# Gated recurrent attention and a two-layer MLP: batches in pairs, every engine on one written-out order, weights loaded later

## The chip, the cores and the metric

One core of one Trainium2 chip. The metric is the device time of one execution in microseconds; the median of several executions is compared. Engines: TensorE (PE, with its weight loads as PEld), VectorE (DVE), ScalarE (ACT), GpSimd (POOL), and SyncE (SP), which here only issues DMAs.

## The reference

A gated linear attention over 4 batches, 8 heads, 768 steps and head width 48, then a leaky-ReLU MLP over the 3072 tokens:

```python
f = 1.0 / (1.0 + np.exp(-f_logit))
for t in range(S):
    state = f[:, :, t, :, None] * state + np.einsum('bhd,bhe->bhde', k[:, :, t], v[:, :, t])
    y[:, :, t] = np.einsum('bhd,bhde->bhe', q[:, :, t], state)
x = np.ascontiguousarray(y.transpose(0, 2, 1, 3)).reshape(B * S, H * D)
h = x @ w_in                      # 384 -> 2048
out = np.maximum(0.01 * h, h) @ w_out   # 2048 -> 384
```

## The kernel before

The recurrence is cut into 6 chunks of 128 steps. A unit is one chunk of one batch with all 8 heads: 128 tokens of width 384, so 24 units, chunk by chunk and in each chunk batch by batch. Inside a chunk the gates become running sums, so that the recurrence turns into matrix products plus one state per batch that goes from chunk to chunk (`state_f` in float32, `state_b` in bf16).

One unit passes through these steps; the names are the functions of the code. `load` issues four 192 KB DMAs (f, k, q, v) on SP. `gate_act` computes log(1 + exp(-f)) on ScalarE; `gate_pe` forms the running sums by a product with a triangle of ones (tile cs); `decay_act` takes exp of plus and minus the sums on ScalarE (em_t, a_t) and the chunk's end factor (a_end). `scale_pool` multiplies k and q by these on POOL (kh, qh) and casts v to bf16 in two layouts. `turn_pe` transposes kh and qh on TensorE into one PSUM tile, and `turn_dve` copies them out (kT, qT). `score_pe` forms k against q per head (tiles pw), `mask_dve` multiplies them by the triangle (wm), and `mix_pe` adds the products with the old state and with v into py, which `y_dve` copies out as xT. `state_pe`, `state_dve` and `state_pool` bring the state forward. The MLP of the unit is `up` (in four groups g of 12 products with 128 columns, each followed by a leaky ReLU on ScalarE into gT), `down` (16 products with 384 columns) and `put` (copy out on VectorE, store on SP).

Each engine works off its own queue in the order in which the code issues to it; the scheduler does not reorder (`manual_schedule`). In turn i of the main loop TensorE gets, in this order: the turns of unit i+1, up groups 0 and 1 of unit i, the scores of unit i+1, the running sums of unit i+2, up groups 2 and 3 of unit i, mix and state of unit i+1, down of unit i. Loads run five units ahead. The weights (w_in in six DMAs, w_out in two, cast to bf16 on the way) are issued on POOL's queue at the start, before the first unit has arrived. PSUM: two banks for up, one for down, one for the turns, two for the scores, two for the rest.

Of the kernel before, what the change touches and what calls it, by code (L numbers as in the profile page):

```python
# [15 lines left out]
def kernel(  # L16
# [21 lines left out]
    units = [(c, b) for c in range(NCH) for b in range(B)]  # L38
    NU = len(units)
# [3 lines left out]
    work = ctx.enter_context(tc.tile_pool(name="work", bufs=3))  # L43
    gpool = ctx.enter_context(tc.tile_pool(name="gpool", bufs=5))
# [10 lines left out]
    nc.scalar.preload_act_table_set("natural_log_exp_and_others")  # L55

# [5 lines left out]
    nc.gpsimd.memset(ones_col, 1.0)  # L62

    w_in_b = const.tile([128, NK, FF], BF16, tag="w_in")
    w_out_b = const.tile([128, NF, KD], BF16, tag="w_out")


    lfs = [const.tile([128, H, 64], BF16, name=f"lf{i}", tag=f"lf{i}") for i in range(3)]
    qhs = [const.tile([128, H, 64], BF16, name=f"qh{i}", tag=f"qh{i}") for i in range(3)]
    khs = [const.tile([128, H, 64], BF16, name=f"kh{i}", tag=f"kh{i}") for i in range(3)]  # L70
    v2s = [const.tile([128, P2, 4, 16], BF16, name=f"v2{i}", tag=f"v2{i}") for i in range(3)]
    state_f = [const.tile([128, P2, D], FP32, name=f"sf{b}", tag=f"sf{b}") for b in range(B)]
    state_b = [const.tile([128, P2, 2 * D], BF16, name=f"sb{b}", tag=f"sb{b}") for b in range(B)]
    for t in lfs + qhs + khs + v2s + state_b:
        nc.vector.memset(t, 0.0)
    for t in state_f:
        nc.vector.memset(t, 0.0)


    raw = {}  # L80

    def load(u):
        c, b = units[u]
        r = {}
        for name, src in (("f", f_logit), ("k", k), ("q", q), ("v", v)):
            t = inp.tile([128, H, D], FP32, name=f"{name}_raw", tag=f"{name}_raw")
            nc.sync.dma_start(out=t, in_=src[b, :, c * C:(c + 1) * C, :].rearrange("h t d -> t h d"))
            r[name] = t
        raw[u] = r

    def load_w_in(part, parts):
        w = FF // parts
        for kk in range(NK):
            nc.gpsimd.dma_start(out=w_in_b[:, kk, part * w:(part + 1) * w],  # L94
                                in_=moe_w_in[kk * 128:(kk + 1) * 128, part * w:(part + 1) * w])

    def load_w_out(part, parts):
        n = NF // parts
        nc.gpsimd.dma_start(  # L99
            out=w_out_b[:, part * n:(part + 1) * n, :],  # L100
            in_=moe_w_out[part * n * 128:(part + 1) * n * 128, :].rearrange("(a p) n -> p a n", p=128))

    st = {}


    def gate_act(u):
        f = raw[u]["f"]
        e = work.tile([128, H, D], FP32, name="e_t", tag="e_t")
        nc.scalar.activation(e, f, AF.Exp, scale=-1.0)  # L109
        lf = lfs[u % 3]  # L110
        nc.scalar.activation(lf[:, :, 0:D], e, AF.Ln, bias=1.0)  # L111

    def gate_pe(u):
        c, b = units[u]
        lf = lfs[u % 3]
        cs = ps_s.tile([128, 512], FP32, name="cs", tag="sm")
        nc.tensor.matmul(cs[:, 0:H * D], ut, lf[:, :, 0:D], start=True, stop=True)  # L117
        if c < NCH - 1:
            for p in range(P2):
                nc.tensor.matmul(cs[:, H * D + p:H * D + p + 1], lf[:, 2 * p:2 * p + 2, :], ones_col,  # L120
                                 start=True, stop=True)
        st[u] = {"cs": cs}

    def decay_act(u):
        c, b = units[u]
        cs = st[u]["cs"]
        a_t = work.tile([128, H, D], BF16, name="a_t", tag="a_t")
        em_t = work.tile([128, H, D], BF16, name="em_t", tag="em_t")
        nc.scalar.activation(em_t, cs[:, 0:H * D], AF.Exp, scale=1.0)  # L129
        nc.scalar.activation(a_t, cs[:, 0:H * D], AF.Exp, scale=-1.0)  # L130
        if c < NCH - 1:
            a_end = work.tile([128, P2], FP32, name="a_end", tag="a_end")
            nc.scalar.activation(a_end, cs[:, H * D:H * D + P2], AF.Exp, scale=-1.0)
            st[u]["a_end"] = a_end
        st[u]["a"], st[u]["em"] = a_t, em_t

    def scale_pool(u):
        r = raw.pop(u)
        nc.gpsimd.tensor_mul(khs[u % 3][:, :, 0:D], r["k"], st[u]["em"])  # L139
        nc.gpsimd.tensor_mul(qhs[u % 3][:, :, 0:D], r["q"], st[u]["a"])  # L140
        v_b = work.tile([128, H, D], BF16, name="v_b", tag="v_b")
        nc.gpsimd.tensor_copy(out=v_b, in_=r["v"])  # L142
        v2 = v2s[u % 3]
        nc.gpsimd.tensor_copy(
            out=v2[:, :, 0:4:3, :],
            in_=r["v"].rearrange("t (p j) d -> t p (j d)", j=2)[:, :, 32:64].rearrange("t p (j e) -> t p j e", j=2))
        st[u]["v"], st[u]["v2"] = v_b, v2

    def turn_pe(u):
        tp = ps_t.tile([128, 2, P2, 128], BF16, name="tp", tag="tp")  # L150
        for i, src in enumerate((khs[u % 3], qhs[u % 3])):
            for p in range(P2):
                nc.tensor.transpose(tp[:, i, p, :], src[:, 2 * p:2 * p + 2, :], ident)  # L153
        st[u]["tp"] = tp

    def turn_dve(u):
        tp = st[u].pop("tp")
        kT = work.tile([128, P2, 128], BF16, name="kT", tag="kT")
        nc.vector.tensor_copy(out=kT, in_=tp[:, 0])  # L159
        qT = work.tile([128, P2, 128], BF16, name="qT", tag="qT")  # L160
        nc.vector.tensor_copy(out=qT, in_=tp[:, 1])  # L161
        st[u]["kT"], st[u]["qT"] = kT, qT

    def score_pe(u):
        kT, qT = st[u].pop("kT"), st[u]["qT"]
        pws = [ps_w.tile([128, P2, 128], FP32, name="pw", tag="pw") for j in range(2)]
        for p in range(P2):
            for j in range(2):
                rows = slice(64 * j, 64 * j + D)
                nc.tensor.matmul(pws[j][:, p, :], kT[rows, p, :], qT[rows, p, :], start=True, stop=True)  # L170
        st[u]["pw"] = pws

    def mask_dve(u):
        st[u]["wm"] = []
        for pw in st[u].pop("pw"):
            wm = work.tile([128, P2, 128], BF16, name="wm", tag="wm", bufs=6)
            nc.vector.tensor_mul(wm, pw, ut[:, None, :].to_broadcast([128, P2, 128]))  # L177
            st[u]["wm"].append(wm)
# [3 lines left out]
    def mix_pe(u):  # L182
        c, b = units[u]
        s = st[u]
        qT, v_b, v2, wms = s.pop("qT"), s["v"], s.pop("v2"), s.pop("wm")
        py = ps_s.tile([128, NK, 128], FP32, name="py", tag="sm")
        jobs = []
        if c > 0:
            for g in range(NQ):
                p, i = divmod(g, 3)  # L190
                jobs.append((g, state_b[b][:, p, 32 * i:32 * i + 32], qT[:, p, :]))
        for j in range(2):
            for p in range(P2):
                jobs.append((3 * p + 2 * j, v_b[:, 2 * p + j, 16 * j:16 * j + 32], wms[j][:, p, :]))
            for p in range(P2):
                jobs.append((3 * p + 1, v2[:, p, 2 * j:2 * j + 2, :], wms[j][:, p, :]))
        left = [sum(1 for g, _, _ in jobs if g % 4 == r) for r in range(4)]
        begun = [False] * 4
        for g, lhsT, rhs in jobs:
            kk, r = divmod(g, 4)  # L200
            left[r] -= 1
            nc.tensor.matmul(py[32 * r:32 * r + 32, kk, :], lhsT, rhs, start=not begun[r], stop=left[r] == 0)  # L202
            begun[r] = True
        s["py"] = py

    def state_pe(u):
        c, b = units[u]
        if c == NCH - 1:
            return
        kh, v_b = khs[u % 3], st[u]["v"]  # L210
        pt = ps_s.tile([128, P2, 2 * D], FP32, name="pt", tag="sm")
        for p in range(P2):
            nc.tensor.matmul(pt[:, p, :], kh[:, 2 * p:2 * p + 2, :], v_b[:, 2 * p:2 * p + 2, :],  # L213
                             start=True, stop=True)
        st[u]["pt"] = pt

    def state_dve(u):
        c, b = units[u]
        if c == NCH - 1:
            return  # L220
# [5 lines left out]
    def state_pool(u):  # L226
        c, b = units[u]
        if c == NCH - 1:
            return
# [127 lines left out]
```

## Time and profile before

| | us |
|---|---|
| median of 3 runs | 209.16 (207.51 to 209.66) |
| span of the profiled execution, first to last instruction | 205.0 |
| TensorE busy in the span | 174.8 (85%) |
| ScalarE, VectorE, POOL busy | 99.5, 90.5, 89.1 |

The page gives no time of the profiled execution beside its span; the median of the runs lies 4.16 us above the span. The page divides the span into 40 slices of 5.1 us; a digit is the busy share of a slice in tenths. Matmuls are pipelined and so overlap in the timeline: the length of a group is read from its start to the start of the next.

### The profile page before, as it was taken

The numbers are of one execution on the slowest core, as the hardware profiler recorded it, in microseconds if no ns is written. First come the engines' busy times: TensorE is split into PE (matmuls) and PEld (weight loads), VectorE is DVE, ScalarE is ACT, GpSimd is POOL, SyncE is SP. The second block draws the span as 40 slices with busy tenths as digits, with TensorE's granted clock in tenths as the row PEclk, the third lists the DMA queues.
The fourth block names the chain that finished last, engine by engine and source line by source line (L and its number), as shares of the span: only waits on it lengthen the run. The fifth ranks groups of instructions, "written<-read, shape, count | busy, mean of one in ns | idle before, by whom it ended". The sixth has DMA issues, their size and how long they took to land.

```text
span 205.0 us, 6488 instructions
## 1 busy us (share of the span) xinstructions
PE 174.8 (85%) x2728; PEld 137.1 (67%) x2728; DVE 90.5 (44%) x204; ACT 99.5 (49%) x213; POOL 89.1 (43%) x173
## 2 busy tenths in 40 slices
PE   0000159999999999999999999999999999999993
PEld 0000039778777877877887787788778777877871
DVE  8000046446445444544544454464445455433511
ACT  4000424466447546635744663574476457444440
POOL 8300183663375357337535633743663474134000
PEclk9999999999999999999999999999999999999999
DMA  6999999899979559557755965785696481110111
GB/s 117 167 196 184 194 189 194 145 218 198 187 139 188 109 118 168 123 125 142 163 125 116 180 141 106 146 176 109 109 190 133 104 156 42 42 38 4 42 38 38
DMA packets 106269, 27.16 MB, mean 132 GB/s; under 512 B 100352, under 2 KB 105472, under 8 KB 106240
## 3 DMA queue, kind: packets, MB, share of 16 engines
q1 hardware_dynamic: 103296, 23.60, 58.8%
q0 software_dynamic: 2944, 3.15, 9.2%
q8 instruction: 21, 0.34, 0.7%
q14 instruction: 8, 0.07, 0.1%
HBM read 25.17 MB, written 4.72 MB: 146 GB/s over the span
## 4 chain that ended last, share of the span: by engine, by line
PE 84%; issue 9%; POOL 4%; DVE 1%; POOLq 0%; DVEq 0%
PE pm L250 32%; PE pm L259 31%; PE py L202 6%; PE tp L153 6%; PE pw L170 4%; PE cs L117 3%; PE pt L213 3%; POOL w_in_b L94 2%; POOL w_out_b L99 1%; PE cs L120 1%; DVE wm L177 1%; POOL kh L139 0%; POOL qh L140 0%; DVE osb L264 0%; DVE kT L159 0%
## 5 line engine op out<-in xcount | busy, mean ns | idle before, releaser
L252 ACT ACTIVATE gT<-pm 128x512 bf16<-128x512 f32 x96 | 56.2, 602 | 73.2 <-PE pm L250 71.4
L250 PE MATMUL pm<-xT,w_in_b 128*128 128x128 bf16 x1152 | 73.0, 221 | 0.0
L250 PEld LDWEIGHTS <-w_in_b 128*128 128x128 bf16 x1152 | 66.8, 98 | 0.6
L259 PE MATMUL pm<-w_out_b,gT 128*128 128x384 bf16 x384 | 66.4, 327 | 0.0
L139 POOL TENSOR_TENSOR kh<-k_raw,em_t 128x384 bf16<-128x384 f32 x24 | 21.9, 913 | 92.5 <-issue 62.5
L259 PEld LDWEIGHTS <-gT 128*128 128x128 bf16 x384 | 36.1, 98 | 22.2
L177 DVE TENSOR_TENSOR wm<-pw,ut 128x512 bf16<-128x512 f32 x48 | 30.9, 686 | 22.1 <-PE pw L170 22.1
L264 DVE COPY osb<-pm 128x384 f32<-128x384 f32 x24 | 13.4, 558 | 45.0 <-PE pm L259 45.0
L117 PE MATMUL cs<-lf,ut 128*128 128x384 bf16 x24 | 8.4, 349 | 23.9 <-ACT lf L111 23.9
L109 ACT ACTIVATE e_t<-f_raw 128x384 f32<-128x384 f32 x24 | 12.4, 516 | 23.8 <-DMA f_raw<-in_f_logit_dram 23.8
L238 DVE CAST xT<-py 128x384 bf16<-128x384 f32 x24 | 13.4, 558 | 21.2 <-PE py L202 21.2
L140 POOL TENSOR_TENSOR qh<-q_raw,a_t 128x384 bf16<-128x384 f32 x24 | 22.0, 915 | 0.0
L120 PEld LDWEIGHTS <-lf 128*128 128x128 bf16 x80 | 5.1, 99 | 24.0 <-issue 22.9
L159 DVE COPY kT<-tp 128x512 bf16<-128x512 bf16 x24 | 10.0, 416 | 22.1 <-PE tp L153 22.0
L234 POOL CAST sb<-sf 64x192 bf16<-64x192 f32 x40 | 13.6, 341 | 2.5
L111 ACT ACTIVATE lf<-e_t 128x384 bf16<-128x384 f32 x24 | 12.6, 524 | 0.8
L129 ACT ACTIVATE em_t<-cs 128x384 bf16<-128x384 f32 x24 | 11.8, 490 | 1.7
L142 POOL CAST v_b<-v_raw 128x384 bf16<-128x384 f32 x24 | 12.1, 504 | 0.0
L130 ACT ACTIVATE a_t<-cs 128x384 bf16<-128x384 f32 x24 | 11.7, 486 | 0.0
L231 POOL TENSOR_TENSOR sf<-sf,a_end 128x192 f32<-128x192 f32 x20 | 10.1, 506 | 3.3 <-DVE sf L224 2.2
L170 PE MATMUL pw<-qT,kT 48*128 48x128 bf16 x192 | 9.8, 223 | 0.8 <-DVE qT L161 0.8
L153 PE MATMUL tp<-ident,kh 128*128 128x128 bf16 x96 | 9.7, 227 | 0.8 <-POOL kh L139 0.8
(37 smaller groups left out, 133.1 us busy)
## 6 DMA issues: line engine op xcount, KB each, us to landing
f_raw<-in_f_logit_dram SPq DMA_DIRECT2D x24, 192.0 KB, 3.3
k_raw<-in_k_dram SPq DMA_DIRECT2D x24, 192.0 KB, 4.0
q_raw<-in_q_dram SPq DMA_DIRECT2D x24, 192.0 KB, 4.3
v_raw<-in_v_dram SPq DMA_DIRECT2D x24, 192.0 KB, 4.6
out_dram<-osb SPq DMA_DIRECT2D x24, 192.0 KB, 2.0
w_in_b<-in_moe_w_in_dram POOLq DMA_DIRECT2D x6, 256.0 KB, 8.9
w_out_b<-in_moe_w_out_dram POOLq DMA_DIRECT2D x2, 768.0 KB, 18.3
```

Source lines behind the costliest of these rows:

```text
L117: nc.tensor.matmul(cs[:, 0:H * D], ut, lf[:, :, 0:D], start=True, stop=True)
L139: nc.gpsimd.tensor_mul(khs[u % 3][:, :, 0:D], r["k"], st[u]["em"])
L140: nc.gpsimd.tensor_mul(qhs[u % 3][:, :, 0:D], r["q"], st[u]["a"])
L153: nc.tensor.transpose(tp[:, i, p, :], src[:, 2 * p:2 * p + 2, :], ident)
L170: nc.tensor.matmul(pws[j][:, p, :], kT[rows, p, :], qT[rows, p, :], start=True, stop=True)
L177: nc.vector.tensor_mul(wm, pw, ut[:, None, :].to_broadcast([128, P2, 128]))
L234: nc.gpsimd.tensor_copy(out=state_b[b][rows, :, j * D:j * D + D], in_=sf[rows])
L238: nc.vector.tensor_copy(out=xT, in_=st[u].pop("py"))
L250: nc.tensor.matmul(pm[:, i, :], w_in_b[:, kk, ff * 128:(ff + 1) * 128], s["xT"][:, kk, :], start=(kk == 0), stop=(kk == NK - 1))
L252: nc.scalar.activation(s["g"][:, 4 * g:4 * g + 4, :], pm, AF.Prelu, alpha=0.01)
L259: nc.tensor.matmul(s["pm2"], s["g"][:, ff, :], w_out_b[:, ff, :], start=(ff == 0), stop=(ff == NF - 1))
L264: nc.vector.tensor_copy(out=osb, in_=st[u]["pm2"])
```

## The change

Two batches of a chunk form a pair, so that there are 12 pairs in place of 24 units. Up runs on a pair: half as many products, with 256 columns each, in eight groups of six products per pair (two of the sixteen blocks of w_in), each with one leaky ReLU of 128x512 as before. Down keeps its products with 384 columns, in quarters of four products per batch. The attention's products per batch stay as they are; turns of k and of q have a PSUM tile each. Four PSUM banks serve cs, turns, scores, py and state sums by turns, up keeps two banks, down gets two. From pair 4 on, the gates and the products and casts of k, q and v are one instruction for both batches (768 columns). For the first pairs k (three pairs) and q (two pairs) are multiplied on VectorE in place of POOL. `half`, `units` and `once` only choose slices and create tiles at first use; `turn_dma` is defined but not used.

The loops are replaced by one table of words, which is worked off from left to right; each word issues one step (`name_pair_batch` or `name_pair_group`) to its engine, so it sets every engine's order. For example `sc_8_2` issues the scores of both batches of pair 8, `up_7_2` the third up group of pair 7, `dn_7_0_0` the first quarter of down of pair 7's first batch, `mk_8_0_1` one mask on VectorE, `pr` a leaky ReLU, `st` a store.

The weights are issued from the table too (`WI_1`, `WO_2`). Each starts with a one-element copy on POOL out of the v tile of the named pair's second batch, so that POOL gets to the weight DMAs only when that load has landed: the 17th load on SP's queue for w_in, the 25th for w_out. w_in comes in two quarters and a half (nine DMAs), w_out in four quarters. The stores stand in SP's queue among the loads.

```diff
-    units = [(c, b) for c in range(NCH) for b in range(B)]
+    pairs = [(c, h) for c in range(NCH) for h in range(B // 2)]
+    BY_UNIT = 4
+    K_DVE = 3
+    Q_DVE = 2
...
-    ps_o = ctx.enter_context(tc.tile_pool(name="ps_o", bufs=1, space=bass.MemoryType.PSUM))
-    ps_t = ctx.enter_context(tc.tile_pool(name="ps_t", bufs=1, space=bass.MemoryType.PSUM))
-    ps_w = ctx.enter_context(tc.tile_pool(name="ps_w", bufs=2, space=bass.MemoryType.PSUM))
-    ps_s = ctx.enter_context(tc.tile_pool(name="ps_s", bufs=2, space=bass.MemoryType.PSUM))
+    ps_o = ctx.enter_context(tc.tile_pool(name="ps_o", bufs=2, space=bass.MemoryType.PSUM))
+    ps_g = ctx.enter_context(tc.tile_pool(name="ps_g", bufs=4, space=bass.MemoryType.PSUM))
...
+    def weights(which, j):
+
+        nc.gpsimd.tensor_copy(out=gate_w[:, 0:1], in_=raw(j, "v")[0:1, 1, H - 1, D - 1:D])
+        if which == "in":
+            for lo, hi in ((0, FF // 4), (FF // 4, FF // 2), (FF // 2, FF)):
+                for kk in range(NK):
+                    nc.gpsimd.dma_start(out=w_in_b[:, kk, lo:hi], in_=moe_w_in[kk * 128:(kk + 1) * 128, lo:hi])
+        else:
+            n = NF // 4
+            for part in range(4):
+                nc.gpsimd.dma_start(
...
+    def half(j, i):
+        return slice(i, i + 1) if j < BY_UNIT else slice(0, 2)
...
+    def scale_k(j, i):
+        a = half(j, i)
+        eng = nc.vector if j < K_DVE else nc.gpsimd
...
+    def up(j, g):
+        pm = st[j]["pm", g] = ps_m.tile([128, 2, 256], FP32, name="pm", tag="pm")
+        for i in range(2):
+            ff = 2 * g + i
             for kk in range(NK):
-                nc.tensor.matmul(pm[:, i, :], w_in_b[:, kk, ff * 128:(ff + 1) * 128], s["xT"][:, kk, :],
+                nc.tensor.matmul(pm[:, i, :], w_in_b[:, kk, ff * 128:(ff + 1) * 128],
+                                 st[j]["xT"][:, kk].rearrange("t a s -> t (a s)"),
                                  start=(kk == 0), stop=(kk == NK - 1))
...
+    order = """
...
+    q_1_0 mx_0_1 tk_1_0 Lq_2_0 sb_0_1 xt_0_1 tq_1_0 pt_1_0 k_1_1 cs_2_0 Lv_2_0 dec_2_0 q_1_1 WI_1 ck_1_0 cq_1_0 tk_1_1
+    gate_2_1 sf_1_0 tq_1_1 ck_1_1 sc_1_0 cq_1_1 cs_2_1 mk_1_0_0 dec_2_1 mk_1_0_1 sc_1_1 up_0_0 mk_1_1_0 v_1_1 mx_1_0
...
+    k_2_1 q_2_1 pr_1_4 up_0_7 Lv_3_0 dec_3_0 tk_2_1 WO_2 tq_2_1 ck_2_1 up_1_5 cq_2_1 pr_0_7 sc_2_2 pr_1_5 up_1_6
+    gate_3_1 mk_2_0_0 mk_2_0_1 up_1_7 pr_1_6 v_2_1 mk_2_1_0 cs_3_1 pr_1_7 mk_2_1_1 pt_2_1 dec_3_1 dn_0_0_0 sf_2_1
+    mx_2_2 Lf_4_0 dn_1_0_0 xt_2_0 sb_2_0 xt_2_1 dn_0_0_1 sb_2_1 dn_1_0_1 up_2_0 k_3_0 pr_2_0 up_2_1 dn_0_0_2 pr_2_1
...
+    tq_8_1 dn_6_1_3 cq_8_1 up_7_1 ob_6_1 q_9_0 sc_8_2 st_6_1 pr_7_1 up_7_2 mk_8_0_0 dn_7_0_0 mk_8_0_1 pr_7_2 up_7_3
+    mk_8_1_0 pt_8_0 pt_8_1 mk_8_1_1 pr_7_3 up_7_4 sf_8_0 mx_8_2 pr_7_4 sf_8_1 up_7_5 sb_8_0 xt_8_0 dn_7_0_1 xt_8_1
...
+    """
+    for word in order.split():
+        name, *numbers = word.split("_")
+        parts[name](*[int(n) for n in numbers])
```

More of the change, by code (lines that the diff above doesn't have):

```diff
@@ L72 @@
[L72 to L118, printed above, removed]
+    for t in v2s:
+        nc.gpsimd.memset(t[:, :, 1:3, :], 0.0)
@@ new lines, in weights @@
+    def weights(which, j):
[8 more added lines that the diff above has]
+                nc.gpsimd.dma_start(
+                    out=w_out_b[:, part * n:(part + 1) * n, :],
+                    in_=moe_w_out[part * n * 128:(part + 1) * n * 128, :].rearrange("(a p) n -> p a n", p=128))
@@ L164, in score_pe @@
[L164 to L178, printed above, removed]
```

374 lines of the change are left out of this document (204 added, 170 removed).

## The prediction

> **What bounds the kernel now.** First the page's busy shares and slices, then the windows cut at TensorE's first layer product and at its last one.
>
> ```profile
> span 205.0 us, 6488 instructions
> ...
> PE   0000159999999999999999999999999999999993
> ...
> DMA  6999999899979559557755965785696481110111
> ```
> ```profile
> 0.00:31.72 31.72, 4.85 (x55) 3.44 (x56) 7.58 (x27) 6.07 (x13) 11.20 (x25) 1.00 1.06 175
> 31.72:201.67 169.95, 169.91 (x2676) 133.69 (x2674) 82.38 (x177) 93.47 (x200) 77.90 (x148) 1.00 0.63 126
> 201.67:205.00 3.33, 0.00 (x0) 0.00 (x0) 0.56 (x1) 0.00 (x0) 0.00 (x0) 0.87 0.16 59
> ```
>
> The columns after the length are busy times of PE, PEld, DVE, ACT and POOL, the clock, the DMA share and GB/s. The span falls into three parts. For 31.72 us TensorE does almost nothing (4.85) while the DMA is full (1.06). Then it is busy for 169.91 of 169.95 us, and no other engine comes near that (ACT 93.47). Then 3.33 us of copying out and storing. So time can come only from the head, from the length of TensorE's own stream, or from new gaps in it. The chain of waits says of the head that it waits for data:
>
> ```profile
> 6.99 17.87 issue
> ...
> 111.50 1.34 PE pm L250 x24
> ...
> 115.66 2.60 PE pm L259 x16
> ```
>
> The stream of one unit, from the timeline (start, length of the piece):
>
> ```profile
> 111.34 1.50 PE L250 MATMUL pm<-xT,w_in_b 128*128 128x128 bf16 x24
> 112.78 0.40 PE L170 MATMUL pw<-qT,kT 48*128 48x128 bf16 x8
> 113.11 0.34 PE L117 MATMUL cs<-lf,ut 128*128 128x384 bf16 x1
> 113.28 0.24 PE L120 MATMUL cs<-ones_col,lf 128*128 128x1 bf16 x4
> 113.38 1.50 PE L250 MATMUL pm<-xT,w_in_b 128*128 128x128 bf16 x24
> 114.81 0.35 PE L202 MATMUL py<-qT,sb 128*32 128x128 bf16 x12
> 114.99 0.23 PE L202 MATMUL py<-wm,v_b 128*32 128x128 bf16 x4
> ...
> 115.50 2.76 PE L259 MATMUL pm<-w_out_b,gT 128*128 128x384 bf16 x16
> 118.10 0.39 PE L153 MATMUL tp<-ident,kh 128*128 128x128 bf16 x4
> ...
> 118.55 1.50 PE L250 MATMUL pm<-xT,w_in_b 128*128 128x128 bf16 x24
> ```
>
> From start to start: 7.21 us per unit, of which up is 1.44 + 1.43 = 2.87, down 2.60, and all attention 1.74.
>
> **The stream in the changed kernel.** The arithmetic stays. Up has half as many products, each with 256 columns in place of 128. Inside a group one with 128 columns takes 1.34 / 24 = 55.8 ns, one with 384 takes 2.60 / 16 = 162.5 ns; the line between gives 109.2 ns for 256, so a unit's 24 take 2.62 us. Of the 2.87 now, 2 x 1.34 = 2.68 is inside groups and 0.19 is the edge to the score and mix products that follow. Inside the groups 0.06 is gained; the edges come once a pair in place of once a unit (0.10 a unit). The gain lies between 24 x 0.06 = 1.4 us and 24 x 0.25 = 6.0 us; I take 24 x 0.155 = 3.7, since score and mix are issued for two units together from pair 2 on.
>
> Before 31.72 TensorE had done unit 0's attention (1.74 less the 0.18 of the state products that the first chunk lacks) and unit 1's sums and turns (0.27 + 0.45), 2.3 us at the steady price. The first layer group was slow:
>
> ```profile
> 31.72 2.35 PE L250 MATMUL pm<-xT,w_in_b 128*128 128x128 bf16 x24
> ...
> 34.61 1.50 PE L250 MATMUL pm<-xT,w_in_b 128*128 128x128 bf16 x24
> ```
>
> That is 0.85 more than the next at the same granted clock. The whole stream after, without it: 169.95 + 2.3 - 0.85 - 3.7 = 167.7 us.
>
> **The head.** All weights now wait for data: w_in for the 17th load on SP's queue, w_out for the 25th. Prices:
>
> ```profile
> 0.74 0.42 SPq L87 DMA_DIRECT2D f_raw<-in_f_logit_dram  x1
> ...
> 3.77 0.52 ACT L109 ACTIVATE e_t<-f_raw 128x384 f32<-128x384 f32 x1 [1.75 <-DMA f_raw<-in_f_logit_dram]
> 4.25 2.40 SPq L87 DMA_DIRECT2D f_raw<-in_f_logit_dram  x1
> 6.69 7.49 SPq L87 DMA_DIRECT2D k_raw<-in_k_dram  x1
> ...
> 26.75 0.81 SPq L87 DMA_DIRECT2D k_raw<-in_k_dram  x1
> ...
> 33.44 0.96 SPq L87 DMA_DIRECT2D f_raw<-in_f_logit_dram  x1
> ```
> ```profile
> q0 software_dynamic: 2944, 3.15, 9.2%
> ...
> v_raw<-in_v_dram SPq DMA_DIRECT2D x24, 192.0 KB, 4.6
> out_dram<-osb SPq DMA_DIRECT2D x24, 192.0 KB, 2.0
> ```
> ```profile
> L94 POOL DMA_DIRECT2D w_in_b<-in_moe_w_in_dram x6: 548/563/744, 1.8 to 4.6; - x6
> ...
> DMA to landing us min/median/max: 4.6/8.9/11.2
> ```
>
> With the DMA full and little of the weights left, seven loads go in 33.44 - 26.75 us: 0.96 each. The first lands by 3.77. So the 17th lands between 3.77 + 16 x 0.96 = 19.1 and 0.74 + 16 x 0.96 + 4.6 = 20.7; I take 20. The weights are 9.2% of 205.0 = 18.9 us of all 16 DMA engines, 9.4 for each matrix, 2.4 for a quarter. While they flowed, five loads went from 4.25 to 26.75: 4.8 of 22.5 us, so the weights had 79%. A quarter then takes 3.0 us, and lands after one issue (0.56) and some 2 us of latency (the store's 2.0): 20 + 0.6 + 3.0 + 2 = 25.6. By the spread of landings (4.6 to 11.2, for twice the bytes) it lies between 24.6 and 31. So the first up starts at 25.5 instead of 31.72, and behind it lies nearly all the attention of two pairs.
>
> Then w_in's second half lands at 20.6 + 9.4 / 0.79 + 2 = 34.5; up(0,4), ninth of sixteen groups, wants it after 9 x 0.66 plus 2 us of attention at about 33.5, so this costs one. The 25th load needs 2.8 + 25 x 0.96 + 9.4 = 36.2 us of full DMA and lands at about 37.5; w_out's quarters land at 43, 46, 49 and 52. TensorE has finished the ups of pairs 0 and 1 and pair 2's attention at about 42. So down waits some 1 us, then goes at the pace of w_out, the gaps filled in part by pair 2's first ups, and ends both pairs at 52 + 1.3 + 0.2 + 5.2 = 58.7. Done by then: ups of four units 10.5, downs 10.4, attention of six units 6 x 1.74 - 4 x 0.18 = 9.7, half of pair 2's ups 2.6, one unit's turns 0.45: 33.7 us. There remain 167.7 - 33.7 = 134.0, to 192.7; with the tail of 3.33, 196.0 us of span.
>
> SP's stores now stand between loads: st(0,0) holds the later loads until about 56, but by then three pairs and the gate inputs of the fourth are loaded, and afterwards a pair needs 8 x 0.96 = 7.7 us of loads in 14 us of TensorE. This I cost at nothing. In the head VectorE takes over k's products (three pairs) and q's (two) from POOL:
>
> ```profile
> L177 DVE TENSOR_TENSOR wm<-pw,ut 128x512 bf16<-128x512 f32 x48 | 30.9, 686 | 22.1 <-PE pw L170 22.1
> L264 DVE COPY osb<-pm 128x384 f32<-128x384 f32 x24 | 13.4, 558 | 45.0 <-PE pm L259 45.0
> ...
> L139 POOL TENSOR_TENSOR kh<-k_raw,em_t 128x384 bf16<-128x384 f32 x24 | 21.9, 913 | 92.5 <-issue 62.5
> ```
> ```profile
> L109 ACT ACTIVATE e_t<-f_raw 128x384 f32<-128x384 f32 x24 | 12.4, 516 | 23.8 <-DMA f_raw<-in_f_logit_dram 23.8
> ...
> L224 DVE TENSOR_TENSOR sf<-sf,pt 64x192 f32<-64x192 f32 x20 | 7.2, 358 | 0.6
> ```
>
> No row shows that product on VectorE; between 0.51 (the mask's rate, 384 of 512 columns) and POOL's 0.91, I take 0.55, nearest to the 558 ns copy of the same width. Eight of them with copies and masks keep VectorE busy until about 21, inside the wait for w_in, so they cost nothing; at 0.91 they add 8 x 0.36 = 2.9 us and use up most of that cover. From pair 4 on ScalarE's gate comes as two instructions of 768 columns, at most 4 x 0.52 = 2.1 us in one piece, with the relus queued behind them and up's two PSUM banks behind those. The table puts three to five quarters of down (0.65 each) at these places, so I cost it at nothing; without that cover it would be 2.1 - 0.66 = 1.4 us in each of eight pairs.
>
> The windows say how this stands to the runs: the shown median of 209.16 lies 4.16 above the profiled span (the page gives that execution no time of its own), which I carry over: 196.0 + 4.2 = 200.2.
>
> Two rules of the Trainium skill speak against parts of this. In the rows, POOL's six issues of w_in, from 1.8 to 4.6 us, took 563 ns each in the median while VectorE ran memsets, the last but one group among them:
>
> ```profile
> 3.74 0.84 DVE L75 MEMSET sb<- 128x192 uint32 x4
> ```
>
> The Trainium skill (SBUF — State Buffer, Who interferes with whom) says that a VectorE instruction in a two-port mode shuts GpSimd out of a shared port, so that descriptors of its DMAs wait. By that rule the nine issues beside VectorE's copies could each wait for one instruction; the six unhindered issues here do not bear it out, and it stands as the third rival. The first group's 2.35 us is what the skill (TensorE: Matmul & The Clock Gate, Part 1) calls the cold clock, to which an idle window returns the array; by that rule each long wait in the new head costs another 0.85 us, 1 to 2 us in sum, which I leave to the range because the page's clock row reads 1.00 here.
>
> **The rivals.** *The weights come in time*: w_in and w_out take nearly the whole DMA while queued, as in the 7.49 us that one load's issue hung, and down never waits. Then TensorE is dense from 25.5 with four units' attention of 1.74 - 0.18 behind it, less some 0.7 that the table puts later: 25.5 + 167.7 - 5.5 + 3.3 = 191.0, 195.2 as a time. Against it: the 25th load must pass w_in first.
>
> *New gaps in every pair.* TensorE works strictly by the table; mix(j) stands behind four masks that take 4 x 0.645 on VectorE and begin 0.43 after the scores:
>
> ```profile
> 163.22 0.40 PE L170 MATMUL pw<-qT,kT 48*128 48x128 bf16 x8
> ...
> 163.65 1.29 DVE L177 TENSOR_TENSOR wm<-pw,ut 128x512 bf16<-128x512 f32 x2 [0.89 <-PE pw L170]
> ```
>
> Masks are done 3.0 us after the scores begin; the table puts 0.66 of scores and about 3.0 of other groups there (pair 8: three ups, a quarter of down, two state sums), some 0.6 us of slack. If a copy out and the state additions (0.56 + 2 x 0.36 us) regularly fall before the masks, and the four shared PSUM banks stay held as long, the stall with its follow-on is up to 1.28 us a pair: 200.2 + 11 x 1.28 = 214. It decides from 8.9 / 11 = 0.8 us a pair. For it: the kernel before had no wait in 169.95 us to spoil. Against it: VectorE is half idle (82.38 of 169.95).
>
> *The head does not get shorter.* Descriptors or queueing delay both matrices by 4.5 us each way (w_in's median landing 8.9 in place of 4.6), and up gains only the 1.4: 200.2 + 4.5 + 2.3 = 207.0, up to 209 if both delays add in part. The change then does not do what its early attention is for.
>
> **The numbers.** Forecast 0.50, weights in time 0.18, new gaps 0.19, head not shorter 0.13. A change of under 1% (2.1 us) cannot be told from none. Faster: 0.50 + 0.18 = 0.68, plus 0.02 of the third rival's lower half: 0.70. Same: 0.11. Slower: 0.19. The range goes from the stall-free head with the larger up gain (195.2 - 2.3, and some 2 for the spread of the runs, 207.51 to 209.66) = 191 to 211, past the third rival and as far as gaps of 1.0 us a pair.
>
> **What would show it.** The first up before 27 us; up pieces of 0.65 us for six products; down's first group after 41; TensorE dense from about 59 and its last product near 193. Wrong it would be if the windows after 60 us show TensorE under 98% busy (the second rival), if the first up comes after 30 us (the third), or if down follows the ups without a gap (the first).

## The result, and the profile after

| us | before | after |
|---|---|---|
| median, runs of one chip | 208.39 (207.51 to 209.66, 4 runs) | 197.58 (196.56 to 198.10, 4 runs) |
| ratio after / before, 95% interval | | 0.946 [0.940, 0.952] |
| span of the profiled execution | 205.0 | 195.7 |
| time of that execution | not given | 197.44 |

Faster by 10.8 us; forecast were 200.2 us of time and 196.0 of span. Ratios leave out executions that took over 1.5% longer than the fastest of their kernel, so a ratio is not always the quotient of the medians beside it.

From the page of the kernel after: busy times, TensorE and its clock and the DMA in 40 slices of 4.9 us, the group of the up products (count, busy us, mean ns, idle before) and the landings of w_in's two quarters (count, KB, us to landing).

```profile
span 195.7 us, 5241 instructions
...
PE   0686379999999999999979999999999999999993
...
PEclk9999999999999999999996999999999999999999
DMA  6999999899999999899999999220001110110112
...
L256 PE MATMUL pm<-xT,w_in_b 128*128 128x256 bf16 x576 | 79.7, 278 | 5.0 <-DMA w_in_b<-in_moe_w_in_dram 3.6
...
w_in_b<-in_moe_w_in_dram POOLq DMA_DIRECT2D x6, 128.0 KB, 6.1
```

Before, TensorE's slices were empty up to the fourth and full from the seventh on. Now they hold work from the second on (the 3 in the fifth is the wait for w_in) and are again full from the seventh, but for one dip, the digit 7 in the 21st slice; the clock's only 6 stands in the slice behind it. Up waited 5.0 us in all, 3.6 of them for w_in. The windows of the kernel after, cut at the first up, the first down, the end of the first downs, around that dip, and at the last product (start:end, length, busy PE, PEld, DVE, ACT, POOL, clock, DMA share, GB/s):

```profile
0.00:24.53 24.53, 12.50 (x138) 8.47 (x139) 16.61 (x41) 12.96 (x31) 14.05 (x37) 1.00 0.98 183
24.53:43.30 18.77, 17.46 (x182) 12.92 (x183) 7.01 (x16) 11.34 (x23) 10.94 (x21) 1.00 1.10 187
43.30:58.00 14.70, 14.64 (x156) 9.77 (x154) 4.57 (x11) 5.29 (x10) 6.80 (x13) 1.00 1.10 199
58.00:95.00 37.00, 37.00 (x524) 28.28 (x522) 22.10 (x49) 23.27 (x46) 20.32 (x30) 1.00 0.99 210
101.00:104.00 3.00, 1.61 (x17) 1.11 (x14) 1.57 (x5) 2.97 (x7) 0.51 (x1) 0.86 1.05 236
104.00:107.00 3.00, 3.00 (x63) 1.91 (x62) 0.34 (x1) 1.59 (x6) 0.86 (x3) 0.57 1.15 228
110.00:150.00 40.00, 40.00 (x538) 30.29 (x537) 22.35 (x48) 19.99 (x40) 17.70 (x27) 1.00 0.40 93
150.00:192.30 42.30, 42.28 (x456) 31.07 (x454) 13.79 (x27) 18.48 (x34) 7.18 (x7) 1.00 0.10 34
192.30:195.70 3.40, 0.00 (x0) 0.00 (x0) 0.56 (x1) 0.00 (x0) 0.00 (x0) 0.94 0.16 58
```

The head is 24.53 us long in place of 31.72, and TensorE is busy for 12.50 us of it in place of 4.85. After 58 us TensorE is without a gap (37.00 of 37.00, 40.00 of 40.00, 42.28 of 42.30) but for the stretch from 101 to 107. The DMA stays full until past 104 us, where in the kernel before it eased after the head (0.63 in the mean): the loads run some four pairs ahead, as fast as the queue takes them.

The steps of the head, from TensorE's timeline of the kernel after (start, length of the piece, in brackets the wait before it):

```profile
24.53 0.40 PE L256 MATMUL pm<-xT,w_in_b 128*128 128x256 bf16 x1 [2.47 <-DMA w_in_b<-in_moe_w_in_dram]
...
26.46 1.03 PE L256 MATMUL pm<-xT,w_in_b 128*128 128x256 bf16 x4 [0.68 <-DMA w_in_b<-in_moe_w_in_dram]
...
27.97 1.46 PE L256 MATMUL pm<-xT,w_in_b 128*128 128x256 bf16 x6
29.36 0.30 PE L225 MATMUL py<-wm,v_b 128*32 128x128 bf16 x4
...
43.32 0.81 PE L267 MATMUL po<-w_out_b,gT 128*128 128x384 bf16 x4
...
51.29 1.46 PE L267 MATMUL po<-w_out_b,gT 128*128 128x384 bf16 x8
52.81 5.36 PE L267 MATMUL po<-w_out_b,gT 128*128 128x384 bf16 x32
58.01 0.39 PE L173 MATMUL tp<-ident,kh 128*128 128x128 bf16 x4
```

The chain that ended last says what sets these steps (start, length, what): the load of q, then POOL's product from it, behind that on POOL's queue the issues of w_out, its transfer, and from then on TensorE.

```profile
21.85 13.14 DMA q_raw<-in_q_dram
35.12 0.91 POOL qh L152
36.16 2.22 POOL w_out_b L111 x3
38.38 12.87 DMA w_out_b<-in_moe_w_out_dram
51.29 1.46 PE po L267 x8
```

And the dip, from the timeline of all engines between 95 and 105 us:

```profile
95.68 2.12 SPq L277 DMA_DIRECT2D out_dram<-osb  x1
...
97.84 0.43 SPq L98 DMA_DIRECT2D f_raw<-in_f_logit_dram  x1
...
100.65 0.84 ACT L121 ACTIVATE e_t<-f_raw 128x768 f32<-128x768 f32 x1 [2.40 <-DMA f_raw<-in_f_logit_dram]
...
102.27 1.07 ACT L262 ACTIVATE gT<-pm 128x512 bf16<-128x512 f32 x2
...
102.90 1.23 PE L256 MATMUL pm<-xT,w_in_b 128*128 128x256 bf16 x6 [1.19 <-ACT gT L262]
...
103.93 1.48 PE L267 MATMUL po<-w_out_b,gT 128*128 128x384 bf16 x4
```

Read it upwards. TensorE waits 1.19 us for a relu; the two relus stand on ScalarE behind pair 9's gate; the gate idles ScalarE for 2.40 us until its load lands; the load was issued at 97.84 because on SP's queue a store stood ahead of it for 2.12 us. When the products go on they are slow: up starts at 102.90 and the next layer product at 103.93, 1.03 us where a group of six takes 0.65, with a granted clock of 0.57 between 104 and 107.

### The profile page after: what moved, and what is told of

The parts are those of the page before. It is cut to its first block, busy times and chain, and to the rows that moved or that the text cites. A ratio compares the mean times of both kernels' runs of the same rounds, so it can differ in the third digit from the quotient of the medians.

```text
span 195.7 us, 5241 instructions
## 1 busy us (share of the span) xinstructions
PE 177.3 (91%) x2152; PEld 130.7 (67%) x2152; DVE 93.4 (48%) x203; ACT 98.4 (50%) x197; POOL 83.3 (43%) x145
## 3 DMA queue, kind: packets, MB, share of 16 engines
q0 software_dynamic: 3408, 3.15, 10.1%
## 4 chain that ended last, share of the span: by engine, by line
PE 69%; DMA 15%; SPq 11%; POOL 2%; issue 1%; ACT 1%; DVE 1%; POOLq 0%
PE po L267 30%; PE pm L256 25%; SPq L98 10%; DMA q_raw<-in_q_dram 7%; DMA w_out_b<-in_moe_w_out_dram 7%; PE py L225 4%; PE tp L173 4%; PE pw L192 2%; DMA f_raw<-in_f_logit_dram 1%; PE cs L127 1%; POOL w_out_b L111 1%; PE pt L236 1%; SPq L277 1%; POOL qh L152 0%; ACT e_t L121 0%
## 5 line engine op out<-in xcount | busy, mean ns | idle before, releaser
L256 PE MATMUL pm<-xT,w_in_b 128*128 128x256 bf16 x576 | 79.7, 278 | 5.0 <-DMA w_in_b<-in_moe_w_in_dram 3.6
L267 PE MATMUL po<-w_out_b,gT 128*128 128x384 bf16 x384 | 75.9, 328 | 0.1
L256 PEld LDWEIGHTS <-w_in_b 128*128 128x128 bf16 x576 | 54.8, 99 | 19.1 <-DMA w_in_b<-in_moe_w_in_dram 4.4
L272 DVE COPY osb<-po 128x384 f32<-128x384 f32 x24 | 13.4, 557 | 40.7 <-PE po L267 40.5
L146 POOL TENSOR_TENSOR kh<-k_raw,em_t 128x768 bf16<-128x768 f32 (+1 forms) x10 | 15.0, 1495 | 15.0 <-ACT em_t L137 8.3
L159 POOL CAST v_b<-v_raw 128x384 bf16<-128x384 f32 (+1 forms) x16 | 10.9, 681 | 23.7 <-DMA v_raw<-in_v_dram 15.7
L152 POOL TENSOR_TENSOR qh<-q_raw,a_t 128x768 bf16<-128x768 f32 (+1 forms) x12 | 16.8, 1399 | 0.5 <-DMA q_raw<-in_q_dram 0.4
L121 ACT ACTIVATE e_t<-f_raw 128x384 f32<-128x384 f32 (+1 forms) x16 | 11.0, 687 | 9.4 <-DMA f_raw<-in_f_logit_dram 9.3
L176 DVE COPY qT<-tp 128x512 bf16<-128x512 bf16 x24 | 9.8, 419 | 5.2 <-PE tp L173 5.0
L122 ACT ACTIVATE lf<-e_t 128x384 bf16<-128x384 f32 (+1 forms) x16 | 10.9, 683 | 0.5
```

Of the source, the lines that this page charges most:

```text
L146: eng.tensor_mul(khs[j % NR][:, a, :, 0:D], raw(j, "k")[:, a], st[j]["em"][:, a].rearrange("t a (h d) -> t a h d", d=D))
L152: eng.tensor_mul(qhs[j % NR][:, a, :, 0:D], raw(j, "q")[:, a], st[j]["a"][:, a].rearrange("t a (h d) -> t a h d", d=D))
L176: nc.vector.tensor_copy(out=turned(j, x)[:, P2 * a:P2 * a + P2, :], in_=st[j].pop(("tp" + x, a)))
L256: nc.tensor.matmul(pm[:, i, :], w_in_b[:, kk, ff * 128:(ff + 1) * 128], st[j]["xT"][:, kk].rearrange("t a s -> t (a s)"), start=(kk == 0), ...
L267: nc.tensor.matmul(po, st[j]["g"][:, ff, 128 * a:128 * a + 128], w_out_b[:, ff, :], start=(ff == 0), stop=(ff == NF - 1))
L272: nc.vector.tensor_copy(out=osb, in_=st[j].pop(("po", a)))
```

## The experiments

The runs came in three groups on different chips; each group has its own runs of the kernel before beside it.

**Weights first, in the changed kernel.** Are the late weights what brings the time? All weight DMAs are issued on POOL at the start, ahead of the memsets, and the words `WI_1` and `WO_2` leave the table.

```diff
+    weights("in", 0)
+    weights("out", 0)
     for t in v2s:
         nc.gpsimd.memset(t[:, :, 1:3, :], 0.0)
...
-        nc.gpsimd.tensor_copy(out=gate_w[:, 0:1], in_=raw(j, "v")[0:1, 1, H - 1, D - 1:D])
...
-    ... cs_2_0 Lv_2_0 dec_2_0 q_1_1 WI_1 ck_1_0 ...
+    ... cs_2_0 Lv_2_0 dec_2_0 q_1_1 ck_1_0 ...
```

> The changed kernel with its weight DMAs issued at the start, without the two copies that hold them back; all else as it is. If the later weights are what lets two pairs' attention run during the loading (the forecast's reading), the 17 loads now stand beside all 18.9 us of weights: the 17th lands at about 2.8 + 17 x 0.96 + 18.9 = 38, TensorE's first up starts at 38 to 41 (24.5 in the changed kernel), the stream is dense from there, and the span is about 40 + 167.7 - 5.5 + 3.3 = 205.5, a time of 205 to 209, about that of the kernel before. If the place of the weights does not matter because the DMA moves the same bytes in any order, first up stays near 25 and the time within 2 us of 197.6.

Measured: 214.19 us (212.90 to 215.53, 4 runs) beside 207.93 before, ratio 1.031 [1.024, 1.038]; span 211.1. From its timeline of TensorE, and then one later wait:

```profile
42.02 1.46 PE L257 MATMUL pm<-xT,w_in_b 128*128 128x256 bf16 x6
...
119.96 0.81 PE L257 MATMUL pm<-xT,w_in_b 128*128 128x256 bf16 x6 [2.03 <-ACT gT L263]
```

The pairs with the weights in the old place are slower than the kernel before: the table wants two pairs' attention ahead of the first up, and their loads crawl beside the weights, so the first up comes at 42.02. From the first up to the last product it takes 165.7 us (42.02 to 207.7), nearly as in the changed kernel from its up at 26.46 (165.8); both stretches have waits in them. The direction was as expected, the size 5 us more than the upper end.

**Weights late, in the kernel before.** The reverse: w_in and w_out behind the second unit's load, nothing else changed.

```diff
     load(0)
-    load_w_in(0, 2)
     load(1)
-    load_w_in(1, 2)
-    load_w_out(0, 2)
-    load_w_out(1, 2)
...
     scale_pool(0)
+    nc.gpsimd.tensor_copy(out=gate_w[:, 0:1], in_=raw[1]["v"][0:1, H - 1, D - 1:D])
+    load_w_in(0, 2)
+    load_w_in(1, 2)
+    load_w_out(0, 2)
+    load_w_out(1, 2)
```

> The kernel before with one edit: the weights are issued after a one-element copy from unit 1's v, behind unit 0's products on POOL, so that two units' loads go first. The loop is unchanged and so only unit 0's attention runs ahead. If the gain of the change needs the attention of two pairs to be run during the loading, little comes of it: two units land by about 2.8 + 8 x 0.96 = 10.5, first up goes at 19 to 21 in place of 31.7, but down of unit 0 waits for w_out until about 31 and 37, and the dense stream begins there: span about 204, 0 to 3 us less than before. If the place of the weights alone brings the gain, the time falls by 7 us or more, to 201 or less.

Measured: 207.26 us (205.68 to 209.07, 10 runs) beside 207.93, ratio 0.996 [0.993, 1.000]. TensorE's timeline of this kernel shows where the gain goes:

```profile
18.93 0.32 PE L250 MATMUL pm<-xT,w_in_b 128*128 128x128 bf16 x1
...
31.76 1.69 PE L259 MATMUL pm<-w_out_b,gT 128*128 128x384 bf16 x8 [2.33 <-DMA w_out_b<-in_moe_w_out_dram]
...
37.09 2.72 PE L259 MATMUL pm<-w_out_b,gT 128*128 128x384 bf16 x8 [3.64 <-DMA w_out_b<-in_moe_w_out_dram]
```

The first up comes 12.8 us earlier, but the fixed order puts down right behind up, and down waits for w_out with nothing else queued that TensorE could do. The time lies within the 0 to 3 us less that were expected. In this execution the granted clock read 0.50 from 34 to 41 us, so the trace is used for the waits only. So the place of the weights is worth less than 1 us by itself and 15.4 us of span (211.1 - 195.7) inside the table, which puts the ups of two pairs and most of a third pair's attention ahead of the first down.

**Up at 128 columns.** The same table, each up product cut in two.

```diff
-            for kk in range(NK):
-                nc.tensor.matmul(pm[:, i, :], w_in_b[:, kk, ff * 128:(ff + 1) * 128],
-                                 st[j]["xT"][:, kk].rearrange("t a s -> t (a s)"),
+            for a in range(2):
+                for kk in range(NK):
+                    nc.tensor.matmul(pm[:, i, 128 * a:128 * a + 128], w_in_b[:, kk, ff * 128:(ff + 1) * 128],
+                                     st[j]["xT"][:, kk, a, :],
```

> The changed kernel with each up product of 256 columns cut into two of 128, one per batch, in the same places. By the row of the kernel before (55.8 ns at 128 columns, 108.7 ns at 256 in the trace of after) an up group goes from 0.65 to 12 x 55.8 = 0.67 us: 96 groups make 1.7 us, a time of 198.5 to 200. If the width carries all of up's shorter time (2.87 us a unit before, 24 products of 108.7 = 2.61 now), it costs 6 us: 203 or more.

Measured: 201.36 us (198.64 to 202.34, 6 runs) beside 207.93, ratio 0.960 [0.953, 0.968]; span 196.9. The median lies above the 198.5 to 200 expected; two of the six executions, the profiled one with 198.64 us among them, lie within. A group takes 0.67 us where it took 0.655, so 96 groups give 1.4 us, and the 76 behind the first downs 1.1. The stream shows about as much: 134.65 us from the end of the first downs to the last product, of which 1.9 are two waits of the dip's kind, leaves 132.75, 1.4 more than the stall-free stream (below) of 131.35. So the width does not carry all of up's shorter time.

**Scores and mix of a pair apart.** In ten pairs the words for scores and mix of both batches become one each, with another step of the table between.

```diff
-    ... cq_2_1 pr_0_7 sc_2_2 pr_1_5 up_1_6 gate_3_1 ...
+    ... cq_2_1 pr_0_7 sc_2_0 pr_1_5 up_1_6 sc_2_1 gate_3_1 ...
```

> The changed kernel with the scores and the mix of pairs 2 to 11 issued for one batch at a time, the second batch's behind the next layer group, so that TensorE goes into and out of these products twice as often. If each entry from a layer group costs 0.10 us, as the forecast put it, 20 more entries cost 2.0 us: 199 to 200. If the edges cost nothing or the masks then come in better time, the time stays within 0.7 us of 197.6.

Measured: 200.06 us (199.74 to 201.90, 6 runs) beside 207.93, ratio 0.965 [0.960, 0.971]; span 198.0. TensorE's timeline of this kernel:

```profile
130.45 0.82 PE L256 MATMUL pm<-xT,w_in_b 128*128 128x256 bf16 x6
131.20 0.40 PE L192 MATMUL pw<-qT,kT 48*128 48x128 bf16 x8
131.53 0.83 PE L256 MATMUL pm<-xT,w_in_b 128*128 128x256 bf16 x6
```

and that of the kernel after, whose scores stand together:

```profile
129.92 0.82 PE L256 MATMUL pm<-xT,w_in_b 128*128 128x256 bf16 x6
130.67 0.62 PE L192 MATMUL pw<-qT,kT 48*128 48x128 bf16 x16
131.22 0.83 PE L256 MATMUL pm<-xT,w_in_b 128*128 128x256 bf16 x6
```

An up group in front of scores takes 0.75 us (130.45 to 131.20) and elsewhere 0.65: the forecast edge of 0.10. But the blocks shrink too: 16 score products together take 0.55 us (130.67 to 131.22), a block of eight by itself 0.33 (131.20 to 131.53), two of them 0.66. Mix shows the same (0.90 together, 0.50 and 0.51 apart). So a split costs 0.10 + 0.11 = 0.21, and 18 splits behind the head 3.8; the stream from the first downs' end to the last product is 135.1 us, 3.75 over the stall-free one.

**The gate of pair 9 later.** The next four ran together, the changed kernel itself among them. If the dip is the gate ahead of the relus, moving its word removes it; the word of pair 10's gate moves back with it.

```diff
-    ... sc_6_2 ob_4_1 up_5_1 mk_6_0_0 st_4_1 gate_9_0 mk_6_0_1 up_5_2 ...
+    ... sc_6_2 ob_4_1 up_5_1 mk_6_0_0 st_4_1 mk_6_0_1 up_5_2 ...
...
-    ... pr_5_7 ck_7_0 up_6_1 gate_10_0 ck_7_1 ...
+    ... pr_5_7 ck_7_0 up_6_1 gate_9_0 ck_7_1 ...
...
-    ... cq_7_1 up_6_2 Lk_11_0 dn_5_1_2 pr_6_2 Lq_11_0 ...
+    ... cq_7_1 up_6_2 Lk_11_0 dn_5_1_2 pr_6_2 gate_10_0 Lq_11_0 ...
```

> The changed kernel as it is, on the same chip as the next three, to compare them with: 196.5 to 198.2. If the wait of up for a relu behind pair 9's gate near 102 us belongs to the table's order, it shows again, between 100 and 105 us; if it was a chance of one run, it does not.

> The changed kernel with two words of the table moved: pair 9's gate on ScalarE to where pair 10's stood, pair 10's a little later. If the 1.2 us gap of TensorE near 102 us, and the slower products for some 3 us behind it, come from that gate waiting for its load with the relus queued behind it, both go: 1.2 to 3 us less than the changed kernel, 194.5 to 196.5. If the late load is only met at the next place, or the gap was hidden otherwise, the time stays within 0.5 us.

Measured: the changed kernel 196.87 us (195.96 to 199.59, 6 runs), with gate 9 later 196.14 (194.21 to 197.15, 6 runs), beside 209.56; ratios 0.941 [0.935, 0.947] and 0.938 [0.932, 0.944]. As times these two cannot be told apart; the traces can. The changed kernel has the wait again, and then runs at full speed:

```profile
105.36 0.81 PE L256 MATMUL pm<-xT,w_in_b 128*128 128x256 bf16 x6 [1.79 <-ACT gT L262]
```

With the gate later, the same group of the table follows without a wait for a relu, and the next layer product comes 0.66 us behind it:

```profile
101.28 0.82 PE L256 MATMUL pm<-xT,w_in_b 128*128 128x256 bf16 x6
101.94 0.81 PE L267 MATMUL po<-w_out_b,gT 128*128 128x384 bf16 x4
```

Its span is 192.4, and from the end of the first downs at 57.72 to the last product at 189.07 it takes 131.35 us. That is the stream without a stall.

The wait stands at this place in seven of the eight traces with the gate at its old place (0.53 to 2.03 us), and in neither of the two with the gate later. The eighth is the run with scores and mix apart: TensorE comes later there, the gate waits only 0.84 us for its load, and TensorE does not wait.

**Keeping TensorE busy until the first up.** 38 products of the identity with itself are put ahead of the first up; nothing reads them.

```diff
+    def warm(n):
+        t = ps_o.tile([128, KD], FP32, name="po", tag="po")
+        for _ in range(n):
+            nc.tensor.matmul(t[:, 0:128], ident, ident, start=True, stop=True)
...
-    ... sc_1_0 cq_1_0 cs_2_1 mk_1_0_0 dec_2_1 mk_1_0_1 sc_1_1 up_0_0 ...
+    ... sc_1_0 cq_1_0 cs_2_1 mk_1_0_0 dec_2_1 mk_1_0_1 sc_1_1 warm_38 up_0_0 ...
```

> The changed kernel with 38 products of 128 columns into an unused PSUM bank (their result is read by nobody) put where TensorE waits for w_in, from about 22.1 to 26.4 us. If the products of 26.4 to 33 us are slow because TensorE sat idle before (a group of six ups takes 1.39 us at first, 0.65 later), they become fast and that stretch shrinks by up to 2.5 us; what comes behind then meets w_out sooner, which landed at about 42.7 with down at 43.3, so the time falls by 0.5 to 2.5 us. If slowness is not due to idleness, or w_out takes all of it back, the time stays within 0.5 us, and the dummies may cost up to 0.7.

Measured: 196.96 us (195.72 to 199.51, 6 runs) beside 209.56, ratio 0.943 [0.937, 0.949]. TensorE's timeline:

```profile
22.41 3.76 PE L273 MATMUL po<-ident 128*128 128x128 bf16 x38
...
28.57 0.83 PE L256 MATMUL pm<-xT,w_in_b 128*128 128x256 bf16 x6
29.33 0.24 PE L225 MATMUL py<-wm,v_b 128*32 128x128 bf16 x4
...
44.27 0.81 PE L267 MATMUL po<-w_out_b,gT 128*128 128x384 bf16 x4 [1.40 <-DMA w_out_b<-in_moe_w_out_dram]
```

Six up products take 0.76 us (28.57 to 29.33) where they took 1.39 in the changed kernel (27.97 to 29.36), so their slowness does come from TensorE's idling. The 38 products are slow themselves, 3.76 us in place of 38 x 55.8 ns = 2.1. It brings nothing: down then waits 1.40 us for w_out, and the first downs end at 59.19 (58.01 and 59.87 in the two traces of the changed kernel). The gap at gate 9 is there too, with 0.53 us.

**Both.** Gate 9 later and the 38 products.

> Both edits together. If they are independent, their gains add: 193 to 196 us. If the head's gain only moves the wait to the loads that lag behind the table, it is no better than the better one alone.

Measured: 195.49 us (194.53 to 195.96, 6 runs) beside 209.56, ratio 0.936 [0.931, 0.941]. The lowest median of the group, but its interval overlaps those of the other three. Put together, the twelve executions with the gate at its old place have a median of 196.93 us and the twelve with it later 195.88; the means of those that the ratios use, 196.83 and 195.53, differ by 1.3 with a standard error of 0.4. So the gate's place does show in the time. In the trace of the run with both edits the stream again takes 131.35 us (59.45 to 190.80), and 1.8 us go to waits for w_out.

**k and q on POOL.** The last two ran together. All products of k and q go back to POOL.

```diff
-    K_DVE = 3
-    Q_DVE = 2
+    K_DVE = 0
+    Q_DVE = 0
```

> The changed kernel with the products of k and q of the first pairs on POOL, as in the kernel before, in place of VectorE. POOL then has 0.9 us more for each of ten products, in the queue ahead of the copy that releases w_in. If VectorE's part keeps POOL's queue free, w_in's release (19.2 us in the changed kernel) comes at 21 to 24, the first up and all behind it by as much later, less what the waits for w_out take back: 1 to 4 us more than the changed kernel. If it costs nothing where it stands, as the forecast put it, and would cost nothing on POOL either, the time stays within 1 us.

Measured: 196.92 us (195.91 to 198.23, 4 runs) beside 208.87, ratio 0.945 [0.937, 0.953]; the changed kernel had 0.946 and 0.941. POOL's copy that releases w_in comes at 19.84 (19.20 in the changed kernel), not at the 21 to 24 of the first reading. The first up starts at 24.54, as it did at 24.53; w_out's issues follow 2.0 us later (38.14 against 36.10), and the last 32 down products of the first two pairs start at 55.49 (54.67 and 52.81 in the changed kernel's traces). What it costs, if anything, lies within the scatter of about 1%.

**w_in from the 13th load.** Its issues wait for the v of pair 1's first batch in place of the second.

```diff
-        nc.gpsimd.tensor_copy(out=gate_w[:, 0:1], in_=raw(j, "v")[0:1, 1, H - 1, D - 1:D])
+        nc.gpsimd.tensor_copy(out=gate_w[:, 0:1], in_=raw(j, "v")[0:1, 0 if which == "in" else 1, H - 1, D - 1:D])
...
-    ... cs_1_1 v_1_0 mk_0_1_1 ... q_1_1 WI_1 ck_1_0 ...
+    ... cs_1_1 v_1_0 WI_1 mk_0_1_1 ... q_1_1 ck_1_0 ...
```

> The changed kernel with w_in released by the 13th load (v of pair 1's first batch) in place of the 17th, at about 15.5 us in place of 19.2. If the head is bound by the bytes that the DMA moves before the scores of pair 1 and before w_out, the first quarter lands 3 us earlier but loads 14 to 17 crawl beside the weights, the first up does not come before 26, w_out still starts near 36, and the time is within 1.5 us of the changed kernel or above it. If the wait for w_in at 22 to 26.5 is what the head costs, it goes, and the time falls by 3 us.

Measured: 196.06 us (194.08 to 198.53, 4 runs) beside 208.87, ratio 0.934 [0.924, 0.943]: not separable from the changed kernel. The four executions took 194.08, 194.46, 197.66 and 198.53 us, and the trace is of the one with 197.66, in which the granted clock falls to 0.50 behind the wait for w_out. Whether the edit is worth some 2 us where the clock stays up, the two short executions do not settle. TensorE's timeline:

```profile
22.89 0.48 PE L127 MATMUL cs<-lf,ut 128*128 128x384 bf16 x1 [2.49 <-ACT lf L122]
...
23.92 1.46 PE L256 MATMUL pm<-xT,w_in_b 128*128 128x256 bf16 x6
...
44.17 1.04 PE L267 MATMUL po<-w_out_b,gT 128*128 128x384 bf16 x4 [3.15 <-DMA w_out_b<-in_moe_w_out_dram]
```

POOL issues w_in 3.5 us earlier (15.81 against 19.33), and up waits for it no more; but the running sums of pair 2, ahead of up in the table, now wait 2.49 us for a gate whose load the weights have pushed back, and down waits 3.15 for w_out, whose issues come 1.0 us later (37.08 against 36.10). In this trace the wait moved twice and was not removed, which fits the first reading, that the bytes the DMA has to move limit the head.

## Why the prediction was right, and where not

| step | forecast | measured, us |
|---|---|---|
| first up | 25.5 | 24.53 |
| up with the third part of the quarter | 25.6 | 26.46 |
| first down | 43 | 43.32 |
| fourth quarter of w_out used | 52 | 51.29 |
| downs of pairs 0 and 1 end | 58.7 | 58.01 |
| from there to the last product | 134.0 | 134.3 |
| tail | 3.33 | 3.4 |
| from the span to the time | 4.16 | 1.74 |

**What bounds it** held: the stream of TensorE was the bound, and the gain came from the head and from the stream. By the forecast's own prices (an estimate) the kernel before has 171.4 us of products (169.95 + 2.3 - 0.85) and loses 30.3 in its head; the kernel after has 165.6 (33.7 + 0.5 + 131.35, see below) and loses 23.8 before the end of the first downs and 3.0 at the dip. So the head gave 6.5 us where 5.3 were forecast, the stream 5.8 where 3.7 were, and the dip took 3.0 back: 9.3 us of span, where 9.0 were forecast. The first two experiments show it from both sides. Neither the weights' place (0.7 us) nor the table with the weights in their old place (6 us slower) does it alone.

**The head** came out within 1 us at each step in this execution. In the second trace of the same kernel the first up starts at 24.50, but the third part of the quarter is used at 28.07, the first down starts at 44.40 and the first downs end at 59.87, up to 2.5 us behind the forecast, so the closeness is in part luck. w_out was released at 36.10, in place of 37.5, and the chain shows POOL's product from the 24th load in front of it, where the forecast named the 25th load alone. The 79% that w_in was given against the loads shows up again; from SP's timeline of the kernel after:

```profile
21.85 3.38 SPq L98 DMA_DIRECT2D q_raw<-in_q_dram  x1
25.27 3.80 SPq L98 DMA_DIRECT2D v_raw<-in_v_dram  x1
29.12 5.05 SPq L98 DMA_DIRECT2D f_raw<-in_f_logit_dram  x1
34.21 0.70 SPq L98 DMA_DIRECT2D k_raw<-in_k_dram  x1
```

Three loads pass in 12.36 us (21.85 to 34.21), worth 2.9 at 0.96 each, which leaves 77% to the weights (an estimate). "Down waits some 1 us" was 0.1 in this trace, and 1.40 and 1.8 with the dummy products.

**VectorE's k and q at nothing** held: they took 570 and 556 ns, where 0.55 us was taken between 0.51 and 0.91, and the run on POOL moved the time by no more than the scatter.

**The stream** was right in its sum by two errors that cancel. The forecast put 134.0 us; the stall-free stream is 131.35. The step that failed there is "the edges come once a pair in place of once a unit", mis-sized: score and mix of two units in one block save not only the entry (0.10 each) but another 0.11 in the block, which is 0.11 x 2 x 9 = 2.0 of the 2.65 us for the nine pairs behind the first downs. Another 0.5 are the running sums of pair 3 (2 x 0.27, at 38.68 and 42.88), which the table puts ahead of the end of the first downs and which the forecast's 33.7 us does not list. The 1.4 us inside the up groups agrees with the experiment at 128 columns.

The other error is the step "the table puts three to five quarters of down at these places, so I cost it at nothing", together with the stores that were to cost nothing among the loads. ScalarE's gate takes 853 + 844 ns, as expected (1.7 us, under the bound of 2.1). At pair 9's gate the table does not have that cover: between this word and the up group that needs the first relu behind it, TensorE has one up group, two state sums and two running sums, some 1.5 us, and no quarter of down. But the price came from the gate's input: the DMA was still full, and the load stood behind a store. The forecast reckoned that "afterwards a pair needs 7.7 us of loads in 14 us of TensorE" and overlooked that loads run some four pairs ahead and keep the DMA full until past 104 us, so that a gate of the table can come before its load. Of the eight gates from pair 4 on, pair 4's waited 2.00 us for its load, pair 7's 0.37 and pair 9's 2.40, the others not at all; at pair 4's TensorE had 32 products of down in hand (52.81 to 58.01) and did not stop. Pair 9's gate cost 1.19 us of waiting and, in this execution, 1.6 us of slow products after it (102.90 to 106.80 are 3.9 us, the same steps with the gate later 101.28 to 103.58, 2.3). Moving the gate took it away. In the new place its load has landed (ScalarE starts it at 109.12 without a wait) and five quarters of down stand in front of the next blocked group, so this experiment does not separate the late load from the missing cover.

**The time.** What was off in the number is the last step, "which I carry over". In every execution that lists both, time and span differ by 1.7 to 1.9 us (197.44 and 195.7), so the profiled execution of before had some 206.8 us (an estimate), less than the 207.51 of the shortest of the runs beside it. Of the 4.16 us carried over 2.4 did not belong there, and that is nearly the whole distance from 200.2 to 197.58. Why before's other executions are longer by that much, no run here shows.

**The rivals.** Weights in time: no; down reached w_out just as it came, and w_in was waited for. The head not shorter: no. POOL's nine issues of w_in took 583 ns in the mean (median 566) beside a VectorE that was busy for 3.35 of the 5.70 us from 19.3 on, where six issues in the kernel before had a median of 563, and a quarter's DMAs landed after 6.1 us, where the forecast had 5.6 (0.6 + 3.0 + 2). The rival rested on a rule of the Trainium skill (SBUF — State Buffer, Who interferes with whom), by which VectorE's two-port copies hold up GpSimd's descriptors. The trace shows no such delay, but it hardly tests the rule: VectorE's instructions in that window are copies and products out of PSUM (kT, qT, wm), and no run here shows whether one of them takes the shared port. New gaps in every pair: behind the first downs the masks brought one gap of 0.20 us (running sums at 101.31 behind wm); the one that cost was of another kind and came once. The clock rule of the Trainium skill (TensorE: Matmul & The Clock Gate, Part 1), by which an idle window returns the array to a cold clock, was kept in the range with 1 to 2 us. The trace agrees in the mechanism, since the dummy products cured the slow ups (1.39 to 0.76 us). To cure it gained no time in the head (196.96 us beside 196.87), where the weights come no sooner.

## What to carry to other kernels

Here moving the weights behind the first data paid only with an order of work that has something to put in the wait that arises for the second weight, and the order paid only with the data first: such edits have to be priced together. When prefetch runs far ahead, ask for every instruction that reads a fresh load whether the DMA is still full at that place, and keep the work that TensorE waits for ahead of it in its queue. Count the cover at each such place in the table, not at a typical one. Carry over only the constant part between span and time; the rest is chance of one execution.

## What the hardware showed that was not expected

- Products that start after the array has idled took 1.39 us for six (after) and 1.40 (weights first) in place of 0.65 to 0.76, while the granted clock of their windows read 1.00 (24.53 to 43.30 after, 42 to 46 weights first). So this row does not show that slowness.
- The wait of 1.19 us at pair 9's gate was followed by a granted clock of 0.57 for 3 us. Waits of 0.53 to 2.03 us at the same place in six other traces were followed by full-speed products, so the wait alone does not explain it. The clock fell behind waits for w_out too: to 0.50 behind 3.64 us (weights late in the kernel before) and behind 3.15 (w_in from the 13th load), and not behind 1.79 (both edits). In 12 of the 34 executions of the kernels whose trace has the wait at the gate the mean granted clock was 0.981 to 0.992; in none of the 18 executions of the three kernels whose trace has none was it under 0.997. So the fall goes with waits in mid-stream; what decides whether it comes stays open.
- The edge between full products and the narrow ones of scores and mix costs 0.10 us on the way in, and a narrow block split in two costs another 0.11.
